# Windowed attention and an ELU feed-forward on one core: the last product's bank copied out by ScalarE, the other sums added from SBUF

## The chip, the cores and the metric

The kernel runs on one core of a Trainium2 chip. The metric is device time in microseconds of one launch. The engines are TensorE (PE, with its weight loads as PEld), VectorE (DVE), ScalarE (ACT), GpSimd (POOL) and SyncE (SP), which issues the DMAs. Each works through its own queue in order and waits on semaphores for the others.

## The reference

For 8 batches and 8 heads, 512 local and 32 global positions, head dimension 64. Global queries see all keys; local queries see the 32 global keys and local keys at most 32 positions away. The 4352 rows of 512 that come out go through two dense layers with an ELU between them.

```python
s_g = scale * q_g @ concat(k_g, k_l).T          # 32 rows per head
out_g = softmax(s_g) @ concat(v_g, v_l)
s_l = concat(scale * q_l @ k_g.T, where(abs(i - j) <= 32, scale * q_l @ k_l.T, -1e9))
out_l = softmax(s_l) @ concat(v_g, v_l)
x = concat(out_g, out_l)                        # to [4352, 512], rows by batch and position
h = x @ w_in                                    # w_in [512, 2048]
g = where(h > 0, h, exp(min(h, 0)) - 1)
out = g @ w_out                                 # w_out [2048, 512]
```

## The kernel before

The rows are worked in 17 blocks of 256 (16 of local rows and one that gathers all global rows). The dense products are done in fp16 parts: each operand is split into a high and a low half, and a product is three matmuls (high by high, high by low, low by high).

For a block, `ffn1` makes 256 columns of h at a time (eight steps `p`): 24 matmuls into a bank called `h`. ScalarE makes `g` (relu, then exp) and `hs` from it, VectorE joins them and forms sums and differences of quarters (`gs`), ScalarE rounds these to the high halves `gh`, and VectorE makes the low halves `gl`. Two steps later `ffn2` takes them to the second product. The first four blocks are done while the weights arrive, in groups of steps, with partial sums parked in DRAM (`od`). The other 13 use `ffn2_seven`: the second product as seven products of 128x128 by 128x256 quarters (Strassen's scheme with sums of quarters), kept over all eight steps in four PSUM banks that stay with it from the first such block on: two of the tiles named `acc`, one named `h`, one named `pa`. Bank `i` holds the products of `SEVEN[i]`, two in each of the first three and the last product alone in `acc[3]` (on rows of the profile: `pa<-cu,gh` and `pa<-cu,gl`). At the last step (`p == NP - 1`) ScalarE copies the first three banks to SBUF tiles `e` (named `tmp`), and functions `s0`, `s1`, `s2` put the four quarters of the output together on VectorE.

PSUM tiles come from three pools: `ps_h` (2 banks), `ps_o` (2) and `ps_a` (4, name `pa`). With `ffn2_seven`'s four taken, one bank is left of `ps_h` and three of `ps_a`; those three serve, in turn, the scores, their transposes, and the product with V.

Attention is a generator of slots that yields between its parts. For each slot `stage_s` (or `stage_ga` for the global rows) makes scores (`pa<-k,q`, `pa<-k,qg`), two slots later `stage_t` transposes the probabilities (`pa<-ident,p`) and VectorE or ScalarE copies them to `pt`, and three slots later `stage_v` multiplies by V (`pa<-pt,v`). For the global rows, `top` finds the maxima (`mg`), `ex` the exponentials `pg` with their sums, and `norm` divides (`sg`, then `pk` and `pg` on GpSimd). `split_x` rounds a finished block of attention output to `xh` and `xl` for ffn1; `scales` makes the factors `xs` of a job on GpSimd; `add_up` forms sums of quarters of w_out (`cu<-wouth,woutl` on GpSimd, then `tmp`).

What orders the work: a loop at the end draws from the attention generator and, by the table `PACE`, from the feed-forward generator, and calls `tick()` after each yield of the latter. `defer(n, fn)` puts `fn` n ticks later. Once the tables of group "f" are there (`pin[0]`), every engine keeps the order in which the program emits; before, a scheduler may reorder. A tick in the middle of the kernel is mostly six matmuls. Most instructions are recorded under line 63, the helper that emits them, so they are told apart by their tiles.

## Time and profile before

| | |
|---|---|
| median of 3 runs | 1060.09 us (1059.58 to 1062.56) |
| profiled execution | 1058.33 us, span 1056.5 us |
| mean granted TensorE clock | 0.975 |
| busy: PE / PEld / DVE / ACT / POOL | 92% / 73% / 75% / 63% / 26% |
| last block without attention beside it | from about 929 us on |
| last matmul, end of the span | about 1043.4 us, 1056.5 us |

A row of a timeline gives the start, the duration in us, engine, line, operation, output<-inputs with shapes and the number of merged instructions; in brackets, how long the engine stood idle before it and what let it go. A row of the waits gives the engine that waited, the one it waited for, the total in us, the number of times and the longest. A row of the groups gives busy time and the mean of one in ns, then idle time ahead. DMA rows are not needed here: the DMA engines' share is low after 400 us.

### The profile page before, as it was taken

Reading aid. Unit: us, or ns where it says so; the run is one execution under the profiler, and the core shown is the slowest. Engines: PE = TensorE matmul, PEld = TensorE weight load, DVE = VectorE, ACT = ScalarE, POOL = GpSimd, SP = SyncE. Lnnn points to the kernel's source line nnn. Section 1 sums busy time; section 2 is a strip of 40 time slices with the busy share of each in tenths; the row PEclk is TensorE's granted clock in tenths of the full one; section 3 lists DMA queues with packets and bytes.
Section 4 is the critical chain, followed back from the end, with each engine's and each line's share of the span. In section 5 each row is a group of like instructions: output and inputs, shape, how many; then the busy total and the mean of one; then the engine's idle time right before and its main releaser. Section 6 shows DMA issues by size and latency. Waiting matters only on the chain.

```text
span 1056.5 us, 21611 instructions
## 1 busy us (share of the span) xinstructions
PE 973.8 (92%) x8128; PEld 776.0 (73%) x8128; DVE 793.2 (75%) x2217; ACT 664.5 (63%) x1535; POOL 271.6 (26%) x458
## 2 busy tenths in 40 slices
PE   6898879887999999989999998999999998999994
PEld 4576546665676688877887787878888887888883
DVE  5789899986886877767776777686886877666663
ACT  4779767764655666555665666566746665656563
POOL 3446484164434321101111121021211221100000
PEclk8899989999999999999999999999999999999998
DMA  7536665430321122002210123012210000000000
GB/s 265 178 109 232 228 218 192 157 116 34 112 65 47 40 76 101 26 11 96 76 46 16 41 76 101 21 35 78 76 41 21 31 21 31 1 21 21 1 21 21
DMA packets 39169, 81.96 MB, mean 78 GB/s; under 512 B 3864, under 2 KB 5912, under 8 KB 39064
## 3 DMA queue, kind: packets, MB, share of 16 engines
q1 hardware_dynamic: 39064, 80.58, 22.7%
q8 instruction: 64, 1.05, 0.4%
q14 instruction: 41, 0.34, 0.1%
HBM read 65.36 MB, written 15.20 MB: 76 GB/s over the span
## 4 chain that ended last, share of the span: by engine, by line
PE 60%; DVE 21%; ACT 11%; issue 3%; POOL 3%; DMA 1%; DVEq 0%; POOLq 0%; ACTq 0%
PE h L63 27%; PE pa L63 20%; PE acc L63 12%; DVE o L63 4%; ACT gh L63 3%; DVE cu L63 3%; DVE gl L63 3%; ACT g L63 2%; DVE g L63 2%; DVE p L63 2%; DVE gs L63 1%; ACT p L63 1%; POOL cu L63 1%; ACT xh L63 1%; DVE woutl L63 1%
## 5 line engine op out<-in xcount | busy, mean ns | idle before, releaser
L63 PE MATMUL h<-xh,winh 128*128 128x256 f16 x992 | 273.6, 276 | 5.8 <-ACT xh L63 5.8
L63 PE MATMUL h<-xl,winh 128*128 128x256 f16 x992 | 273.3, 276 | 0.1
L63 PE MATMUL h<-xh,winl 128*128 128x256 f16 x992 | 273.2, 275 | 0.0
L63 POOL TENSOR_SCALAR p<-p,sm 128x224 f32<-128x224 f32 x256 | 139.7, 563 | 466.8 <-DVE sm L63 273.2
L63 PEld LDWEIGHTS <-winh 128*128 128x128 f16 x2176 | 213.3, 99 | 44.9 <-issue 14.2
L63 PEld LDWEIGHTS <-gh 128*128 128x128 f16 x1712 | 166.7, 99 | 68.6 <-issue 29.0
L63 ACT ACTIVATE g<-h,xs 128x512 f32<-128x512 f32 x124 | 85.0, 686 | 178.2 <-PE h L63 178.0
L63 DVE SCALAR_TENSOR_TENSOR gl<-g,xs,gh 128x256 f16<-128x256 f32 (+1 forms) x136 | 81.5, 599 | 96.8 <-ACT gh L63 96.1
L63 ACT ACTIVATE p<-p,m 128x224 f32<-128x224 f32 x256 | 120.7, 478 | 16.1 <-DVE m L63 15.7
L63 PEld LDWEIGHTS <-winl 128*128 128x128 f16 x1088 | 107.5, 99 | 13.8 <-issue 0.4
L63 PE MATMUL acc<-wouth,gh 128*128 128x256 f16 (+1 forms) x336 | 109.1, 325 | 7.9 <-DVE o L63 6.5
L63 PEld LDWEIGHTS <-gl 128*128 128x128 f16 x856 | 83.9, 98 | 34.7 <-DVE gl L63 6.9
L63 PE MATMUL acc<-wouth,gl 128*128 128x256 f16 (+1 forms) x336 | 106.3, 316 | 2.6 <-DVE gl L63 2.5
L63 PE MATMUL acc<-woutl,gh 128*128 128x256 f16 (+1 forms) x336 | 106.2, 316 | 0.0
L63 DVE TENSOR_TENSOR gs<-g 128x256 f32<-128x256 f32 (+1 forms) x312 | 102.1, 382 | 3.6
L63 DVE SCALAR_TENSOR_TENSOR gl<-gs,xs,gh 128x640 f16<-128x640 f32 x104 | 92.8, 893 | 15.9 <-ACT gh L63 15.5
L63 DVE SCALAR_TENSOR_TENSOR g<-g,hs 128x512 f32<-128x512 f32 x136 | 97.7, 719 | 4.8 <-ACT g L63 4.8
L63 ACT ACTIVATE gh<-g,xs 128x256 f16<-128x256 f32 (+1 forms) x136 | 75.5, 555 | 33.3 <-DVE g L63 32.4
L63 PE MATMUL pa<-ident,p 128*128 128x128 f32 x512 | 79.6, 282 | 14.0 <-ACT pg L63 5.8
L63 ACT ACTIVATE gh<-gs,xs 128x640 f16<-128x640 f32 x104 | 85.6, 823 | 2.0 <-DVE gs L63 1.9
L63 ACT ACTIVATE g<-g 128x512 f32<-128x512 f32 x136 | 85.5, 629 | 0.0
L63 ACT ACTIVATE hs<-h,xs 128x512 f32<-128x512 f32 x124 | 84.4, 681 | 0.0
(169 smaller groups left out, 1812.5 us busy)
## 6 DMA issues: line engine op xcount, KB each, us to landing
v<-vT SPq DMA_DIRECT2D x64, 256.0 KB, 2.7
k<-kT SPq DMA_DIRECT2D x32, 448.0 KB, 3.6
out<-o SPq DMA_DIRECT2D x34, 256.0 KB, 2.2
q<-qT SPq DMA_DIRECT2D x32, 256.0 KB, 5.3
raw<-w_in SPq DMA_DIRECT2D x8, 1024.0 KB, 6.5
raw<-w_out SPq DMA_DIRECT2D x8, 1024.0 KB, 5.1
od<-o SPq DMA_DIRECT2D x24, 256.0 KB, 2.3
o<-od SPq DMA_DIRECT2D x24, 256.0 KB, 3.2
```

The source lines that it names most:

```text
L63: ins = getattr(self.engine, name)(*args, **kwargs)
```

## The change

At the last step ScalarE also copies the bank of the last product, scaled, into two quarters of the output tiles (`c11` and `c22`) as soon as its matmuls are issued. VectorE forms the remaining sums in the SBUF tiles `m4` and `m6` and adds these to `c11` and `c22`; before, it read the bank itself in the last two operations. The output tiles are taken at that earlier point. And for global rows `ex` and `norm` are deferred by 3 and 6 ticks rather than 4 and 7.

```diff
                 if p == NP - 1 and i < 3:
                     nc.scalar.activation(e[i].rearrange("p a b -> p (a b)"), acc[i], AF.Copy, scale=oc)
+                elif p == NP - 1:
+                    o = [ffn.tile([P, DM], F32, name="o", bufs=3) for _ in range(2)]
+                    c11, c12, c21, c22 = (o[t][:, c:c + 256] for t in range(2) for c in (0, 256))
+                    for c in (c11, c22):
+                        nc.scalar.activation(c, acc[3][:, 0:256], AF.Copy, scale=oc)
                 yield
             if p == NP - 1:
-                o = [ffn.tile([P, DM], F32, name="o", bufs=3) for _ in range(2)]
                 (m6, m3), (m7, m4), (m2, m5) = ((x[:, 0, :], x[:, 1, :]) for x in e)
-                c11, c12, c21, c22 = (o[t][:, c:c + 256] for t in range(2) for c in (0, 256))
 
                 def s0():
+                    nc.vector.tensor_add(c21, m2, m4)
                     nc.vector.tensor_sub(c12, m5, m3)
-                    nc.vector.tensor_sub(c11, m4, m7)
-                    nc.vector.tensor_sub(c11, c11, m5)
+                    nc.vector.tensor_sub(m4, m4, m7)
 
                 def s1():
-                    nc.vector.tensor_sub(c22, m6, m3)
-                    nc.vector.tensor_sub(c22, c22, m2)
-                    nc.vector.tensor_add(c21, m2, m4)
+                    nc.vector.tensor_sub(m4, m4, m5)
+                    nc.vector.tensor_sub(m6, m6, m3)
+                    nc.vector.tensor_sub(m6, m6, m2)
 
                 def s2():
-                    for t, c in enumerate((c11, c22)):
-                        nc.vector.scalar_tensor_tensor(out=c, in0=acc[3][:, 0:256], scalar=oc, in1=c,
-                                                       op0=ALU.mult, op1=ALU.add)
+                    for t, (c, m) in enumerate(((c11, m4), (c22, m6))):
+                        nc.vector.tensor_add(c, c, m)
                         nc.sync.dma_start(out_rows(blk, t), o[t])
...
             if pin[0]:
-                for i, fn in ((1, top), (4, ex), (7, norm)):
+                for i, fn in ((1, top), (3, ex), (6, norm)):
                     defer(i, fn)
```

TensorE's order is the same in both. VectorE at the end of the first seven-product block (near 410 us; `tmp` are the copied banks, `o` the output tiles, `pt` the transposed probabilities, `mg` the maxima of global rows):

```order
 L63 TENSOR_TENSOR o<-tmp 128x256 x2
-L63 TENSOR_TENSOR o<-o,tmp 128x256
-L63 TENSOR_TENSOR o<-tmp 128x256
-L63 TENSOR_TENSOR o<-o,tmp 128x256
-L63 TENSOR_TENSOR o<-tmp 128x256
-L63 COPY pt<-pa 128x4x128
-L63 SCALAR_TENSOR_TENSOR o<-pa,xs,o 128x256 x2
+L63 TENSOR_TENSOR tmp<-tmp 128x256 x4
+L63 COPY pt<-pa 128x4x128
+L63 TENSOR_TENSOR o<-o,tmp 128x256 x2
 L63 TENSOR_REDUCE mg<-pa 128x1 x2
```

The eight operations stay eight and keep their places, ahead of and behind the copy to `pt`; the last two no longer name the bank `pa`. On ScalarE the two copies `o<-pa` stand behind `tmp<-h`, at most a few exponentials `p` or copies `pt` and `xr` later. ScalarE's order near 452 us, before and then after:

```order
L63 ACTIVATE gh<-g,xs 128x256
L63 ACTIVATE gh<-gs,xs 128x640
L63 ACTIVATE xh<-xr,xm 128x1024
L63 ACTIVATE pg,sg<-pa,mg 128x272 x2
L63 COPY pt<-pa 128x4x32
```

```order
L63 ACTIVATE gh<-g,xs 128x256
L63 ACTIVATE gh<-gs,xs 128x640
L63 ACTIVATE pg,sg<-pa,mg 128x272 x2
L63 ACTIVATE xh<-xr,xm 128x1024
L63 COPY pt<-pa 128x4x32
```

`pg` and `xh` change places here and near 572 us; at the other six global rows' places after 405 us they keep theirs. GpSimd's order near 330 us (`xs` are the scales of the first seven-product job, `cu` sums of w_out's quarters):

```order
 L63 MEMSET pt 96x4x32
-L63 TENSOR_SCALAR xs<-isc,xm 128x8 x2
-L63 TENSOR_SCALAR xs<-t_f,xm 128x8
-L63 TENSOR_SCALAR xs<-wm_f,xm 128x1
-L63 TENSOR_SCALAR pk<-pg,sg 128x32
-L63 TENSOR_SCALAR pg<-pg,sg 128x4x128
+L63 TENSOR_SCALAR pk<-pg,sg 128x32
+L63 TENSOR_SCALAR pg<-pg,sg 128x4x128
+L63 TENSOR_SCALAR xs<-isc,xm 128x8 x2
+L63 TENSOR_SCALAR xs<-t_f,xm 128x8
+L63 TENSOR_SCALAR xs<-wm_f,xm 128x1
 L63 TENSOR_TENSOR cu<-wouth,woutl 128x1024 x2
```

The scales move behind `pk` and `pg`. Near 300 us one `cu` moves behind `pk` and `pg` in the same way.

## The prediction

> **What bounds the kernel now.** I read the page's busy time first, then the list of who waited for whom (TensorE's part), then the timeline of each engine around every place where TensorE stood still after 405 us.

> ```profile
> PE 973.8 (92%) x8128; PEld 776.0 (73%) x8128; DVE 793.2 (75%) x2217; ACT 664.5 (63%) x1535; POOL 271.6 (26%) x458
> PE pa L63 <- DVE o L63: 13.5, 10, 3.0
> ```

> TensorE is the bound. Its longest wait in total is the one that the change aims at: ten times, 13.5 us together, the first matmul into bank `acc[3]` (tile `pa`) of a new block stood until VectorE had done the last two operations on `o`, which read that bank. In the stage without attention three of these waits follow one another:

> ```profile
> 929.19 0.38 PE L63 MATMUL pa<-cu,gh 128*128 128x256 f16 x2 [1.19 <-DVE o L63]
> ...
> 970.32 0.38 PE L63 MATMUL pa<-cu,gh 128*128 128x256 f16 x2 [1.35 <-DVE o L63]
> ...
> 1011.45 0.38 PE L63 MATMUL pa<-cu,gh 128*128 128x256 f16 x2 [1.35 <-DVE o L63]
> 965.74 0.70 ACT L63 ACTIVATE tmp<-h,xs 128x512 f32<-128x512 f32 x1
> ```

> **Term 1, the boundaries without attention: -3.9 us.** ScalarE finished `tmp<-h` of the boundary at 970 at 965.74 + 0.70 = 966.44, and in the new order the two copies of bank 3 come next on it. Nothing shows these copies; the nearest rows are a copy of the same size out of PSUM and, as an upper end, the 128x512 one above (0.70 each):

> ```profile
> L63 ACT COPY xr<-pa 128x256 f32<-128x256 f32 x54 | 20.4, 378 | 17.0 <-PE pa L63 17.0
> L63 DVE TENSOR_TENSOR o<-o,tmp x26: 424/425/569, 411.2 to 1045.4; 128x256 f32<-128x256 f32 x26
> L63 DVE SCALAR_TENSOR_TENSOR o<-pa,xs,o x26: 453/472/479, 413.4 to 1046.5; 128x256 f32<-128x256 f32 x26
> ```

> I take 0.38 each, since size and source are the same, so 0.75 for both (at most 1.4). The bank is then free at about 967.2 to 967.8. TensorE comes to it at 970.32 - 1.35 = 968.97 without the wait, so nothing of the wait is left: 1.19 + 1.35 + 1.35 = 3.9 us. ScalarE's own 0.75 us per block lies in time in which it is ahead of TensorE here. VectorE runs eight operations as before; the two that read PSUM (0.472) become adds from SBUF (0.425), about 0.1 us less per block, at most 0.15 each more where an add runs as the slowest one above (0.569).

> **Term 2, the boundaries with attention: -4.5 us of 9.6.** 13.5 - 3.9 = 9.6 us of the waits lie there, in seven places. After `acc[3]` TensorE comes to the product with V (`pa<-pt,v`), at once or after half of an ffn1. That product needs the second `pt` copy of VectorE: it reads it, and its output takes the bank that the copy empties. VectorE issues this copy next to the same `o` operations. So TensorE is let go by `o` only to meet `pt`. Pairs of copy and product, boundary by boundary, VectorE's and then TensorE's timeline:

> ```profile
> 475.91 0.68 DVE L63 COPY pt<-pa 128x512 f32<-128x512 f32 x1
> ...
> 533.46 0.67 DVE L63 COPY pt<-pa 128x512 f32<-128x512 f32 x1
> ...
> 594.80 0.67 DVE L63 COPY pt<-pa 128x512 f32<-128x512 f32 x1
> ...
> 653.20 0.68 DVE L63 COPY pt<-pa 128x512 f32<-128x512 f32 x1
> ...
> 711.27 0.68 DVE L63 COPY pt<-pa 128x512 f32<-128x512 f32 x1
> ...
> 768.15 0.66 DVE L63 COPY pt<-pa 128x512 f32<-128x512 f32 x1
> ...
> 881.16 0.66 DVE L63 COPY pt<-pa 128x512 f32<-128x512 f32 x1
> ```

> ```profile
> 477.84 1.21 PE L63 MATMUL pa<-pt,v 128*64 128x160 f32 x16
> ...
> 534.19 1.21 PE L63 MATMUL pa<-pt,v 128*64 128x160 f32 x16
> ...
> 595.52 1.21 PE L63 MATMUL pa<-pt,v 128*64 128x160 f32 x16
> ...
> 654.41 1.21 PE L63 MATMUL pa<-pt,v 128*64 128x160 f32 x16
> ...
> 712.48 1.21 PE L63 MATMUL pa<-pt,v 128*64 128x160 f32 x16
> ...
> 769.72 1.21 PE L63 MATMUL pa<-pt,v 128*64 128x160 f32 x16
> ...
> 881.01 0.38 PE L63 MATMUL pa<-cu,gh 128*128 128x256 f16 x2 [3.04 <-DVE o L63]
> ...
> 882.74 1.21 PE L63 MATMUL pa<-pt,v 128*64 128x160 f32 x16
> ```

> At 534.19 and 595.52 the product already starts 0.06 and 0.05 us after the copy's end (534.13, 595.47): there the gain is only what VectorE is sooner, 0.15 each. Elsewhere the gain is the product's start less the copy's end and 0.06: 477.84 - 476.65 = 1.2; 654.41 - 653.94 = 0.5; 712.48 - 712.01 = 0.5; 769.72 - 768.87 = 0.85; 882.74 - 881.88 = 0.85. With 0.1 us less on VectorE at the last four, 1.2 + 0.15 + 0.15 + 0.6 + 0.55 + 0.95 + 0.9 = 4.5 us. At 881 the wait of 3.04 us thus turns into one of some 2.1 us on `pt`. The ends: 0, where the next thing on VectorE binds as well, and 9.6. ScalarE's 0.75 us is covered here too: it makes `g`, `hs`, `gh` later by that much, and their readers (`gl` on VectorE, and TensorE when it reuses the only free `h` bank) come later than that, with the least to spare at 881, where `hs` would end about when TensorE wants the bank; there TensorE is to wait for `pt` anyway. The output DMAs on SP stand behind the same last operations as before.

> **Term 3, the softmax of the global rows one tick sooner: -4.7 us.** ScalarE's order changes at two of the eight places after 405 us: `xh` now comes behind the two `pg` activations (at 452 and 572).

> ```profile
> 446.84 0.77 DVE L63 TENSOR_REDUCE mg<-pa 128x1 f32<-128x272 f32 x2
> 451.17 1.15 ACT L63 ACTIVATE xh<-xr,xm 128x1024 f16<-128x1024 f32 x1 [1.59 <-DVE xm L63]
> 452.22 0.47 ACT L63 ACTIVATE pg<-pa,mg 128x272 f32<-128x272 f32 x1
> 452.93 0.82 PE L63 MATMUL pa<-ident,p 128*128 128x128 f32 x4 [2.34 <-ACT pg L63]
> ...
> 572.57 0.99 PE L63 MATMUL pa<-ident,p 128*128 128x128 f32 x4 [2.35 <-ACT pg L63]
> ```

> The maxima (`mg`) were long there; ScalarE stood 1.59 us for `xm` with `pg` queued behind. In the new order `pg` runs in that idle time, from about 449.6, and frees TensorE's bank by 450.3, before TensorE wants it (452.93 - 2.34 = 450.59). `xh` still starts when `xm` is there, with room for the two `pg` ahead of it. So both waits go: 2.34 + 2.35 = 4.7 us, unless VectorE's next `pt` copy, which is not sooner, holds TensorE in turn (then down to 0):

> ```profile
> 455.60 0.67 DVE L63 COPY pt<-pa 128x512 f32<-128x512 f32 x1
> ```

> ```profile
> 459.52 1.03 PE L63 MATMUL pa<-k,q 64*128 64x224 f32 x8
> ```

> It ends at 456.27; the scores that need its bank come at 459.52 - 2.34 = 457.18 or later, 0.9 us behind it, so I keep the whole.

> **Term 4, GpSimd's queue: +1.0 us.** The same edit puts `pk` and `pg` on GpSimd ahead of the first seven-product job's scales (`xs`).

> ```profile
> 329.82 1.33 POOL L63 TENSOR_SCALAR xs<-isc,xm 128x8 f32<-128x8 f32 x2
> ...
> 331.36 0.26 POOL L63 TENSOR_SCALAR xs<-wm_f,xm 128x1 f32<-128x1 f32 x1
> 338.43 0.29 POOL L63 TENSOR_SCALAR pk<-pg,sg 128x32 f32<-128x32 f32 x1 [6.81 <-DVE sg L63]
> ...
> 341.94 0.69 DVE L63 TENSOR_TENSOR tmp<-cu 128x512 f32<-128x512 f32 x1 [2.68 <-POOL cu L63]
> ```

> The scales ran in GpSimd's idle time; now they wait behind `pk` for `sg`, and `cu`, for which VectorE already stood 2.68 us, comes behind them. They took 331.62 - 329.82 = 1.8 us, the last of the four 0.26: 1.0 to 1.8 for four. VectorE, which has hardly a gap for some 15 us from there, then holds TensorE through `pt`. I take 1.0 (0 to 2.7, a repeat of VectorE's wait). At the other place where GpSimd's order changes (`cu` behind `pk`, `pg` near 300 us) TensorE shows no wait, so I put nothing. The tail, after the last matmul, gains 0.1.

> **Sum:** -3.9 - 4.5 - 4.7 + 1.0 - 0.1 = -12.2 us. The profiled execution took 1058.33 us (span 1056.5) and would take 1046.1. It is 1.8 us under the median of the runs, 1060.09; against that I forecast 1047.9 us.

> [...] GpSimd's `p` scalings run beside these VectorE operations at several boundaries:

> ```profile
> L63 POOL TENSOR_SCALAR p<-p,sm 128x224 f32<-128x224 f32 x256 | 139.7, 563 | 466.8 <-DVE sm L63 273.2
> ```

> The dependent adds from SBUF quoted above, some of them beside such scalings, took 0.569 at the worst and 0.425 in the median. [...]

> **The rivals.**
> 1. *All of the waits go*: VectorE also gets to `pt` sooner, or the product was not bound by it. Then -13.5 - 4.7 + 1.0 - 0.1 = -17.3, 1042.8 us. For it: the group row. Against: the two starts 0.05 us behind the copy.
> 2. *The waits in the attention stages only change their name*: `pt` and other VectorE work hold TensorE there for as long, and what is won at 452 and 572 is given back to `pt`. Only the stage without attention gains: -3.9 - 0.1 + 1.0 = -3.0, 1057.1 us. For it: VectorE is busy without a gap around each boundary. Against: it has gaps later in every block.
> [...]

> **Chances.** The forecast 0.58; rival 1 0.12; rival 2 0.15; rival 3 0.10, of which 0.04 for the part that makes it slower; 0.05 for none of these. What this kernel's measurement can tell from no change is about 0.3%, 3.2 us, so rival 2 lies at its edge. Faster 0.83, same 0.11, slower 0.06. The range goes from rival 1 to beyond rival 3 with one scaling and near rival 2: 1042.5 to 1055.5 us.

> **What would show it.** Right: no wait of `pa` for `o` on TensorE; one for `pt` that grows from little to some 4 us, the largest at the boundary near 870; the three late blocks 39.8 us apart instead of 41.1; no wait of TensorE for `pg` near 450 and 560. Wrong: adds of `o` over 0.6 us (rival 3), TensorE waiting for `hs` or `gl` after a boundary (ScalarE's 0.75 us not covered), or a wait of over 2 us near 340 (term 4 too small).

## The result and the profile after

| | before | changed |
|---|---|---|
| median of four runs each, us | 1060.62 (1059.58 to 1062.56) | 1046.75 (1044.79 to 1048.67) |
| ratio of times, 95% interval | | 0.9867 (0.9843 to 0.9891) |
| profiled execution, us | 1058.33 | 1044.79 |
| its span, us | 1056.5 | 1043.0 |

The forecast was 1047.9 us, 12.2 us less than before; the profiled execution became 13.5 us shorter. From the page of the changed kernel, the busy time, and from the list of waits TensorE's rows (us in total, times, the longest):

```profile
PE 970.9 (93%) x8128; PEld 774.2 (74%) x8128; DVE 790.9 (76%) x2217; ACT 673.9 (65%) x1561; POOL 273.4 (26%) x458
PE pa L63 <- DVE pt L63: 9.0, 13, 1.4
PE pa L63 <- ACT pg L63: 1.1, 1, 1.1
```

The row "pa <- DVE o" (13.5 us, ten times) no longer exists. ScalarE has 26 instructions and 9.4 us more, the copies of the bank. Two rows that the prediction did not show stood in the kernel before as follows:

```profile
PE pa L63 <- DVE pt L63: 2.0, 3, 1.4
PE pa L63 <- ACT pg L63: 5.8, 3, 2.4
```

So 13.5 us of waits for `o` and 4.7 for `pg` went, and 7.0 us of waits for `pt` came; 5.35 of these stand at the product with V behind the boundaries, where the prediction expected some 4. TensorE's timeline shows some of the new waits at that product, and, last, the uses of the bank in the stage without attention, which have no wait in brackets any more and are 39.62 us apart (41.13 before):

```profile
343.48 0.77 PE L63 MATMUL pa<-pt,v 128*64 128x160 f32 x8 [0.57 <-DVE pt L63]
...
475.55 1.21 PE L63 MATMUL pa<-pt,v 128*64 128x160 f32 x16 [1.35 <-DVE pt L63]
...
872.64 0.71 PE L63 MATMUL pa<-pt,v 128*64 128x160 f32 x8 [0.59 <-DVE pt L63]
...
874.17 0.71 PE L63 MATMUL pa<-pt,v 128*64 128x160 f32 x8 [0.82 <-DVE pt L63]
...
958.40 0.38 PE L63 MATMUL pa<-cu,gh 128*128 128x256 f16 x2
...
998.02 0.38 PE L63 MATMUL pa<-cu,gh 128*128 128x256 f16 x2
```

**Where the time went, piece by piece.** TensorE runs the same 8128 matmuls in the same order in both kernels, so the n-th of one can be set against the n-th of the other. The change of the difference of their starts over a stretch is what the stretch gained or lost. In us, by stretches of the kernel before; the last two rows are the first two experiments below:

| against before | 0-300 | 300-400 | 400-500 | 500-600 | 600-700 | 700-800 | 800-900 | 900-end |
|---|---|---|---|---|---|---|---|---|
| changed kernel | -0.5 | +2.33 | -4.13 | -3.18 | -0.59 | -1.54 | -1.46 | -4.36 |
| bank copy only | -3.0 | +1.59 | -0.92 | -0.32 | -0.57 | -1.53 | -1.45 | -4.35 |
| ticks only | +0.4 | +2.32 | -1.62 | -2.86 | +0.01 | +0.02 | +1.61 | +0.02 |

The first column is what executions differ by anyway: two kernels below that are the same up to 405 us differ by up to 2.6 us there. Behind 300 us stretches that run the same work agree to 0.02 us, so that one profiled execution resolves tenths of a microsecond there, with one exception: up to 405 us the kernel with the bank copy only is the kernel before, and yet it lost 1.59 us between 300 and 400 us. It has a window at half the TensorE clock there (near 360 us) that the kernel before has not; such windows come up again below, and a single execution can have one more or one less of them. The changed kernel gained 12.9 us behind 300 us: +2.33 (term 4), -6.05 (term 3: -3.19 around 452 and -2.86 around 572, and the ticks alone show the same two), -4.85 (term 2, what is left of 400 to 900; the bank copy alone shows 4.8) and -4.36 (term 1).

### The profile page after: what moved, and what is told of

Same layout as the page of the kernel before. It is cut to its first block, busy times and chain, and to the rows that moved or that the text cites. A ratio compares the mean times of both kernels' runs of the same rounds, so it can differ in the third digit from the quotient of the medians.

```text
span 1043.0 us, 21668 instructions
## 1 busy us (share of the span) xinstructions
PE 970.9 (93%) x8128; PEld 774.2 (74%) x8128; DVE 790.9 (76%) x2217; ACT 673.9 (65%) x1561; POOL 273.4 (26%) x458
## 4 chain that ended last, share of the span: by engine, by line
PE 60%; DVE 22%; ACT 11%; issue 3%; POOL 3%; DMA 1%; SPq 0%; DVEq 0%; POOLq 0%; ACTq 0%
PE h L63 27%; PE pa L63 21%; PE acc L63 13%; DVE cu L63 3%; DVE gl L63 3%; ACT gh L63 3%; DVE g L63 2%; ACT g L63 2%; DVE tmp L63 2%; DVE p L63 2%; ACT p L63 1%; DVE gs L63 1%; DVE o L63 1%; POOL cu L63 1%; DVE xl L63 1%
## 5 line engine op out<-in xcount | busy, mean ns | idle before, releaser
L63 PE MATMUL h<-xh,winh 128*128 128x256 f16 x992 | 271.6, 274 | 5.8 <-ACT xh L63 5.8
L63 PE MATMUL h<-xl,winh 128*128 128x256 f16 x992 | 271.3, 274 | 0.1
L63 PE MATMUL h<-xh,winl 128*128 128x256 f16 x992 | 271.3, 273 | 0.0
L63 POOL TENSOR_SCALAR p<-p,sm 128x224 f32<-128x224 f32 x256 | 142.7, 577 | 456.0 <-DVE sm L63 257.5
L63 PEld LDWEIGHTS <-winh 128*128 128x128 f16 x2176 | 211.8, 99 | 43.8 <-issue 14.4
L63 PEld LDWEIGHTS <-gh 128*128 128x128 f16 x1712 | 166.9, 99 | 54.5 <-issue 13.7
L63 ACT ACTIVATE g<-h,xs 128x512 f32<-128x512 f32 x124 | 85.1, 687 | 168.0 <-PE h L63 164.9
L63 DVE SCALAR_TENSOR_TENSOR gl<-g,xs,gh 128x256 f16<-128x256 f32 (+1 forms) x136 | 82.3, 605 | 88.9 <-ACT gh L63 88.2
L63 ACT ACTIVATE p<-p,m 128x224 f32<-128x224 f32 x256 | 120.7, 478 | 15.7 <-DVE m L63 15.3
L63 PE MATMUL acc<-wouth,gh 128*128 128x256 f16 (+1 forms) x336 | 109.1, 325 | 8.7 <-DVE o L63 6.6
L63 PEld LDWEIGHTS <-winl 128*128 128x128 f16 x1088 | 106.8, 98 | 13.1 <-issue 0.4
L63 PEld LDWEIGHTS <-gl 128*128 128x128 f16 x856 | 84.1, 98 | 35.2 <-DVE gl L63 7.4
L63 PE MATMUL acc<-wouth,gl 128*128 128x256 f16 (+1 forms) x336 | 106.3, 316 | 3.1 <-DVE gl L63 3.0
L63 PE MATMUL acc<-woutl,gh 128*128 128x256 f16 (+1 forms) x336 | 106.2, 316 | 0.0
L63 DVE TENSOR_TENSOR gs<-g 128x256 f32<-128x256 f32 (+1 forms) x312 | 102.1, 381 | 3.6
L63 DVE SCALAR_TENSOR_TENSOR gl<-gs,xs,gh 128x640 f16<-128x640 f32 x104 | 92.6, 890 | 15.5 <-ACT gh L63 15.1
L63 DVE SCALAR_TENSOR_TENSOR g<-g,hs 128x512 f32<-128x512 f32 x136 | 96.0, 706 | 4.6 <-ACT g L63 4.6
L63 ACT ACTIVATE gh<-g,xs 128x256 f16<-128x256 f32 (+1 forms) x136 | 75.9, 558 | 31.6 <-DVE g L63 30.8
L63 ACT ACTIVATE gh<-gs,xs 128x640 f16<-128x640 f32 x104 | 86.0, 827 | 2.5 <-DVE gs L63 2.4
L63 PE MATMUL pa<-ident,p 128*128 128x128 f32 x512 | 79.4, 280 | 8.5 <-POOL p L63 3.4
L63 ACT ACTIVATE g<-g 128x512 f32<-128x512 f32 x136 | 85.9, 631 | 0.0
L63 ACT ACTIVATE hs<-h,xs 128x512 f32<-128x512 f32 x124 | 84.7, 683 | 0.0
```

The source lines that it names most:

```text
L63: ins = getattr(self.engine, name)(*args, **kwargs)
```

## The experiments

**1. The bank copy alone.** The changed kernel with the ticks of before:

```
-                for i, fn in ((1, top), (3, ex), (6, norm)):
+                for i, fn in ((1, top), (4, ex), (7, norm)):
```

> Only the bank copy, its sums and adds; the exponentials of the global rows and their normalisation stay at ticks 4 and 7. Theory (the parts add, each as the two traces show it): the three late boundaries give 1.3 + 1.5 + 1.5 = 4.3 us, the seven in attention 4.3 us net, the tail 0.1: 8.7 us under the kernel before, about 1051.9 us. The waits of TensorE for `pg` near 452 and 572 us stay at 2.3 us each, and so do the two spells at half clock right behind them. Rival (the two parts need each other: with the exponentials behind `xh` the second copy on ACT delays them further): the pg waits grow by up to 0.9 us at each boundary and the gain shrinks to 5 us or less, about 1055.5 us.

Measured: 1049.83 us (1047.63 to 1051.7), ratio 0.9904 (0.9888 to 0.992) against 1059.73 us for the kernel before on this chip. The list of waits and TensorE's timeline at the place near 452:

```profile
PE pa L63 <- ACT pg L63: 5.8, 3, 2.3
```

```profile
451.49 0.85 PE L63 MATMUL pa<-ident,p 128*128 128x128 f32 x4 [2.34 <-ACT pg L63]
```

The waits for `pg` are as long as before, and the half-clock windows behind them are there (451.8 and 571.2 us). The late blocks gave 4.35 us and 400 to 900 us gave 4.8, against 4.3 expected of each. The theory holds; the rival falls. The 1.59 us between 300 and 400 us are not the copies' doing, as said above.

**2. The ticks alone.** The kernel before, with `(3, ex), (6, norm)`; the bank is read as before.

> Only the ticks: exponentials of the global rows at tick 3 and their normalisation at tick 6, the bank read as before. Theory: the two waits for `pg` near 452 and 572 us go, and with each the half-clock window behind it, in all 6.5 us; GpSimd's queue near 340 us costs 2.1 us back, part of it a new half-clock window near 364 us: 4.4 us under the kernel before, about 1056.2 us. Rival (the half-clock windows come and go by chance and do not belong to the wait): only the waits go, 4.7 us less 1 us, and the two half-clock windows are seen again near 453 and 573 us: 3.7 us or less, 1056.9 us.

Measured: 1058.67 us (1054.12 to 1060.41, 12 runs), ratio 0.9986 (0.9974 to 0.9998): nearly nothing. Both expectations missed the time. The waits for `pg` and the half-clock windows at 453 and 573 us are gone, as the theory said, and the cost near 340 is the same +2.32. But two waits that the kernel has always had are now followed by half-clock windows, which they were not before. Here is the one near 477 us, in windows of 3.41 us by the clock record's own borders (time, length, busy time and instructions of PE, PEld, DVE, ACT, POOL, then the granted clock). First the kernel before, then the ticks alone, and last TensorE's timeline of the ticks alone:

```profile
473.70:477.11 3.41, 1.52 (x12) 1.07 (x11) 3.34 (x9) 1.13 (x3) 2.82 (x4) 1.00 0.00 0
477.11:480.53 3.42, 3.10 (x34) 2.55 (x34) 3.38 (x13) 1.68 (x8) 0.00 (x0) 1.00 0.55 195
```

```profile
473.86:477.27 3.41, 1.21 (x10) 0.72 (x8) 3.38 (x10) 0.47 (x1) 2.29 (x4) 1.00 0.00 0
477.27:480.69 3.42, 3.42 (x24) 2.56 (x23) 3.35 (x12) 2.14 (x8) 0.00 (x0) 0.50 0.52 164
```

```profile
476.93 0.38 PE L63 MATMUL pa<-cu,gh 128*128 128x256 f16 x2 [2.20 <-DVE o L63]
```

The wait for `o` is the same (2.20 us here, 2.21 before). Before, a border cut it, and the window held 3.41 - 1.52 = 1.89 us of idle time; here it lies inside one window, 2.20 us, and the next window ran at a clock of 0.50. At 881 us the wait of 3.04 us does the same (1.92 us of it in one window before, 2.62 now). The table shows the price: 400 to 500 us gives 1.6 instead of 3.2, and 800 to 900 loses 1.61. With the 2.32 us near 340 they eat what the ticks gained. One of the 12 executions took 1054.12 us at a mean granted clock of 0.978, against 0.971 in the profiled one, so not every execution has as many half-clock windows. In the changed kernel these two waits do not exist. So the two parts of the change do need each other, though in another way than I had thought of: the ticks are worth 0.5 us alone and 5.4 us on top of the bank copy (both in the traces behind 300 us; 3.8 us if the bank copy's trace had not had its own window near 360 us).

**3. The normalisation back at tick 7**, the exponentials left at tick 3.

```
-                for i, fn in ((1, top), (3, ex), (6, norm)):
+                for i, fn in ((1, top), (3, ex), (7, norm)):
```

> The changed kernel with the normalisation back at tick 7 and the exponentials left at tick 3, so that GpSimd scales `xs` ahead of `pk` and `pg` again in front of the first job of seven products. Theory (the term of GpSimd's queue cost 2.1 us there): the wait of ACT for `xs` near 339 us falls from 3.0 us to under 1 us, the half-clock window near 364 us goes, the waits for `pg` at 452 and 572 us stay away since ACT's order decides them: 2 us under the changed kernel, about 1044.7 us. Rival (the tick of the normalisation is what brought `pg` in time): 2.4 to 3.2 us come back at each of 452 and 572 us, and the kernel is 2 to 4 us over the changed one, 1049 us or more.

Measured: 1042.55 us (1042.05 to 1045.52), ratio 0.9842 (0.9824 to 0.986); against the changed kernel's trace -2.33 us between 300 and 400 us and 0.00 to the end. ScalarE's row in the changed kernel and in this one:

```profile
339.33 0.69 ACT L63 ACTIVATE g<-h,xs 128x512 f32<-128x512 f32 x1 [3.01 <-POOL xs L63]
```

```profile
336.94 0.69 ACT L63 ACTIVATE g<-h,xs 128x512 f32<-128x512 f32 x1 [1.02 <-PE h L63]
```

The wait for `xs` and TensorE's 0.57 us for `pt` at 343 are gone, and with them the half-clock window at 364. The wait for `gl` in front of that window is the same length in both kernels:

```profile
362.17 0.28 PE L63 MATMUL acc<-wouth,gl 128*128 128x256 f16 x1 [2.03 <-DVE gl L63]
```

```profile
361.07 0.28 PE L63 MATMUL acc<-wouth,gl 128*128 128x256 f16 x1 [2.01 <-DVE gl L63]
```

What differs is where it falls: one window holds 2.07 us of idle time in the changed kernel and 1.36 here. It does not look like chance: with the exponentials early, the four traces with GpSimd's new order (the changed kernel, 2, 4 and 6) hold 2.07 to 2.10 us there and all have the window, the five with the old order (3, 5, 7, 8 and 9) hold 1.30 to 1.46 and none has it. But it is not the kernel alone that decides: with both ticks as before, the kernel before has none there (1.20 us), and the bank copy alone, the same program up to there, has one (2.16 us idle in the window, its +1.59 in the table). The waits for `pg` stay away: ScalarE's order decides them.

**4. The sums later.** The changed kernel, with the three groups of sums nine ticks further back:

```
-                    defer(1 + i, fn)
+                    defer(10 + i, fn)
```

> The changed kernel with the three groups of sums put off by nine ticks more, behind the `pt` copies and `gl` on VectorE. Theory (what is late after the change is `pt`, behind the sums of VectorE: 5.35 us of waits of V at the seven boundaries in attention): most of these waits go, 3 to 5 us under the changed kernel, about 1043 us. Rival (`pt` is late because of the softmax chain itself, or the sums now stand in front of something as urgent, `gl` or the next `o`): 0 to 1 us, or slower by up to 2 us through waits for `gl` or `o` that are not there now.

Measured: 1040.77 us (1038.99 to 1042.57), ratio 0.9819 (0.9801 to 0.9837); against the changed kernel's trace -6.25 us behind 300 us, all of it between 400 and 900. VectorE's timeline at the first boundary, in the changed kernel and in this one, and this one's row in the list of waits:

```profile
472.11 0.18 DVE L63 RECIPROCAL sm<-sm 128x4 f32<-128x4 f32 x1
472.20 0.74 DVE L63 TENSOR_TENSOR o<-tmp 128x256 f32<-128x256 f32 x2
472.86 2.03 DVE L63 TENSOR_TENSOR tmp<-tmp 128x256 f32<-128x256 f32 x4
474.82 0.68 DVE L63 COPY pt<-pa 128x512 f32<-128x512 f32 x1
```

```profile
473.62 0.18 DVE L63 RECIPROCAL sm<-sm 128x4 f32<-128x4 f32 x1
473.71 0.66 DVE L63 COPY pt<-pa 128x512 f32<-128x512 f32 x1
```

```profile
PE pa L63 <- DVE pt L63: 3.6, 6, 1.4
```

The copy that TensorE waits for came 2.71 us behind the reciprocal because six sums, which nobody was waiting for, stood between. Put off, they cost nothing: the waits for `pt` fall from 9.0 to 3.6 us, none of them is at V behind a boundary, and no wait for `gl` or `o` takes their place. The gain is above the 3 to 5 us expected.

**5. Both together** (experiments 3 and 4).

> The sums put off and the normalisation back at tick 7, both in the changed kernel. Theory (two separate places: V behind `pt` at the seven boundaries, ACT behind `xs` near 339 us): the two gains add, 2.6 us (with no half-clock window near 364 us) under the kernel with the late sums alone: about 1038.5 us, and no half-clock window between 270 us and the end. Rival (with the sums behind `gl` the normalisation at tick 7 finds VectorE busy and `pg` comes late): no better than the late sums alone, 1040.8 us or more.

Measured: 1036.77 us (1036.01 to 1038.97), ratio 0.9797 (0.9783 to 0.9811) against 1058.26 us on this chip; -8.55 us against the changed kernel's trace behind 300 us (-2.32 and -6.23). The clock record shows no half-clock window between 268 and 1025 us. The gains add, and this is the fastest version that was run.

**6. The copies made twice.** The changed kernel:

```
-                    for c in (c11, c22):
+                    for c in (c11, c22, c11, c22):
```

> The changed kernel with both copies of the bank made twice, two more ACT instructions of 0.36 us pitch at each of 13 ends, which also hold the bank 0.7 us longer. Theory (the copies lie beside TensorE's work; between the second copy's end and the next use of the bank near 919 us there are 1.8 us): within 1 us of the changed kernel, and the late blocks stay 39.6 us apart. Rival (ACT's chain behind the copies, `g`, `hs`, `gh`, or the exponentials in attention, comes last): each of the ten binding ends pays up to 0.7 us, 4 to 7 us in all, the late blocks 40.3 us apart.

Measured: 1047.26 us (1046.68 to 1048.26), ratio 0.9894 (0.988 to 0.9907), an interval that overlaps the changed kernel's. The traces are sharper: behind 300 us TensorE's matmuls differ by 0.01 us from the changed kernel's, in sum and in each stretch. Near 870 TensorE first waits 0.6 us for `hs`, and then as much less for `pt`. ScalarE's copies are covered at all 13 ends, and made twice they still cost nothing; near 870 that is so only because `pt` comes later still.

**7. VectorE reads the bank first**, on top of experiment 5; no copies on ScalarE.

```
-                    for c in (c11, c22):
-                        nc.scalar.activation(c, acc[3][:, 0:256], AF.Copy, scale=oc)
+                    for c, m in ((c11, e[1][:, 1, :]), (c22, e[0][:, 0, :])):
+                        nc.vector.scalar_tensor_tensor(out=c, in0=acc[3][:, 0:256], scalar=oc, in1=m,
+                                                       op0=ALU.mult, op1=ALU.add)
```

> On top of the late sums with tick 7: no ACT copies; VectorE reads the bank at once instead, adding M4 and M6 as it does (c11 = bank + M4, c22 = bank + M6), and the other sums are taken from the output tile later. Theory (what counts is that the bank is read first, by whichever engine): within 1.5 us of the kernel with both, about 1038 us; ACT has 0.85 us less at each end. Rival (VectorE's two reads of some 0.55 us stand ahead of `g`, `gs` and `gl`, or behind other work of VectorE, so that the bank is let go later): 0.5 to 1 us at each of ten ends, 1043 to 1048 us.

Measured: 1038.34 us (1037.55 to 1039.06), ratio 0.9807 (0.9794 to 0.982). Against experiment 5's trace it is +1.33 us behind 300 us, at one place: the scores at 585 us, which wait for VectorE's `sm`, behind the two reads.

```profile
585.06 0.99 PE L63 MATMUL pa<-k,q 64*128 64x224 f32 x6 [1.58 <-DVE sm L63]
```

So what counts is that the bank is read first, and hardly which engine does it; ScalarE, with more room, is the slightly better one.

**8 and 9. Waits made on purpose.** On top of experiment 5, each pair of copies is repeated so that ScalarE holds the bank longer, by another amount at each of the 13 ends; `n` counts the ends.

```
-                    for c in (c11, c22):
+                    n = state["n7"] = state.get("n7", -1) + 1
+                    for c in (c11, c22) * (1 + (2, 3, 4, 5)[n % 4]):
```

> A kernel made to wait: late sums with tick 7, and the pair of bank copies repeated 2, 3, 4, 5, 2, 3, ... times more at the 13 ends, so that ACT holds the bank 1.4 to 3.6 us longer and TensorE idles for graded times there (time 1045 to 1065 us; only the trace counts). Theory (the clock is set by fixed windows of 3.41 us; one in which TensorE idles for about 2.0 us or more is followed by one at half clock): each wait of over 2.0 us inside one window is followed by a half-clock window that costs up to 1.7 us, and a wait of the same length that is cut by a window's border is not. Rival 1 (only a window that is idle from end to end counts): no half-clock window behind any wait under 3.4 us. Rival 2 (no tie to waits): half-clock windows stand where TensorE did not wait, as often as behind waits. [...]

Measured: 1050.49 us (one run). The waits came out shorter than meant, 1.9 us at most for `o` and no window after 265 us with over 1.55 us of idle time; no half-clock window appeared. That agrees with the theory and with rival 1, and tells nothing apart, so the series was made longer, with (5, 6, 7, 8, 9)[n % 5]:

> The same made longer: the pair of copies repeated 5, 6, 7, 8, 9, 5, ... times more at the 13 ends, so that the bank is let go 3.6 to 6.5 us later and TensorE waits for `o` for 1.5 to over 4 us (time 1060 to 1095 us; only the trace counts). By the windows counted in the runs so far the next window ran at half clock whenever TensorE was idle for 2.07 us or more of one (nine windows after 265 us), and never when it was idle for 1.92 us or less. Theory (that share decides, wherever in the window the idle time lies): every window after 265 us with over 2.1 us of idle time is followed by a half-clock one, none with under 1.9 us is, and waits of the same length fall on either side by where the border cuts them. Rival (only a window that is idle from end to end): half-clock windows only behind waits that hold a whole window, over 3.4 us, at most a few here.

Measured: 1092.47 us (one run). Four windows, each with the one behind it:

```profile
657.43:660.84 3.41, 0.74 (x6) 0.51 (x6) 0.00 (x0) 3.41 (x10) 0.00 (x0) 1.00 0.03 11
660.84:664.26 3.42, 3.42 (x24) 2.36 (x22) 2.48 (x7) 1.39 (x4) 0.00 (x0) 0.50 0.00 0
...
995.34:998.75 3.41, 1.52 (x14) 1.13 (x12) 0.00 (x0) 3.41 (x10) 0.00 (x0) 1.00 0.00 0
998.75:1002.17 3.42, 3.36 (x31) 2.77 (x30) 1.85 (x3) 3.01 (x6) 0.00 (x0) 1.00 0.00 0
```

```profile
473.11:476.52 3.41, 1.54 (x19) 1.16 (x18) 0.29 (x3) 3.41 (x9) 0.23 (x1) 1.00 0.00 0
476.52:479.94 3.42, 3.42 (x19) 2.43 (x18) 2.65 (x5) 3.30 (x12) 0.00 (x0) 0.50 0.26 81
...
950.97:954.38 3.41, 0.00 (x0) 0.00 (x0) 0.00 (x0) 3.41 (x11) 0.00 (x0) 1.00 0.00 0
954.38:957.80 3.42, 2.77 (x14) 1.98 (x14) 0.49 (x2) 3.38 (x7) 0.00 (x0) 0.50 0.02 5
```

All six windows at full clock with 2.14 to 3.41 us of idle time (2.28 at 592.57, 2.67 at 657.43 and 3.41 at 950.97 among them) were followed by one at half clock, and only the one at 950.97 is idle from end to end: the rival falls. The border is not sharp: 1.87 us (473.11) was enough, against what I expected, and 1.89 us (995.34) was not.

## Why the prediction held, and where its steps failed

**Term 1 (boundaries without attention): -4.36 us, forecast -3.9.** Mechanism and place as forecast. The three waits gave 1.35, 1.51 and 1.51 us, 0.16 more each than their rows (1.19, 1.35, 1.35). The reason is how a wait is counted:

```profile
968.70 0.27 PE L63 MATMUL h<-wouth,gl 128*128 128x256 f16 x1
970.32 0.38 PE L63 MATMUL pa<-cu,gh 128*128 128x256 f16 x2 [1.35 <-DVE o L63]
```

```profile
958.29 0.27 PE L63 MATMUL h<-wouth,gl 128*128 128x256 f16 x1
958.40 0.38 PE L63 MATMUL pa<-cu,gh 128*128 128x256 f16 x2
```

The wait is counted from the modelled end of the matmul ahead, 968.70 + 0.27. Without it the next one starts 0.11 us after that matmul's start, as the changed kernel's second pair shows: 1.62 - 0.11 = 1.51. A matmul's printed length is not its pitch, the time from one start to the next.

**Term 2 (boundaries with attention): -4.85 us, forecast -4.5.** The reading that TensorE is let go by `o` only to meet `pt` was right: of 9.6 us of waits for `o` about half was gained. This is shown, not only argued, by experiment 4, which took the cause of the new waits away and gained another 6.25 us. The shares were less exact than the sum: 0.94 us at 477 instead of 1.2, and 1.47 at 881 instead of 0.9; the other five came within 0.03. At 477 VectorE's six sums ahead of `pt` had become slower. They took 2.35 us from their first start to the copy's before (473.56, below, to 475.91) and 2.62 in the changed kernel (472.20 to 474.82), which is the 0.26 us that are missing:

```profile
473.56 0.74 DVE L63 TENSOR_TENSOR o<-tmp 128x256 f32<-128x256 f32 x2
```

Rival 1 (all of the waits go) needed the sums out of `pt`'s way, which this change did not do; in experiment 4 the seven places gave 11.1 us together, which is all of their waits when each is counted as in term 1.

**Term 3 (softmax of the global rows): -6.05 us, forecast -4.7.** Both waits went, as said, and gave 2.5 us each. Two sizes failed. The window behind each wait had run at half clock, which the prediction did not look for. In the kernel before and in the changed one:

```profile
453.22:456.64 3.42, 3.42 (x19) 2.48 (x17) 2.95 (x9) 0.32 (x3) 0.79 (x2) 0.50 0.00 0
```

```profile
453.00:456.40 3.40, 3.40 (x33) 3.10 (x32) 2.18 (x3) 2.93 (x6) 0.00 (x0) 1.00 0.00 0
```

At half clock 19 matmul instructions fit, at full clock 33; that was 1.7 us at each place. And "I keep the whole" was wrong. TensorE comes to the scores 4.2 us sooner, not 2.34, and so ahead of the `pt` copy, which is not sooner. VectorE's and then TensorE's timeline in the changed kernel:

```profile
457.44 1.27 DVE L63 COPY pt<-pa 128x512 f32<-128x512 f32 x2
```

```profile
458.17 1.02 PE L63 MATMUL pa<-k,q 64*128 64x224 f32 x6 [0.37 <-DVE pt L63]
```

The waits for `pt` are 0.37 us here and 0.71 near 573 by their rows, and by the starts 1.00 and 1.35 us were given back.

**Term 4 (GpSimd's queue): +2.3 us, forecast +1.0.** What the term named, V's wait for `pt`, cost 0.7 us; VectorE's wait for `cu` grew by only 0.3 us, to 2.98. The rest, 1.6 us, is the half-clock window at 364, which this small delay triggered by moving a wait of 2.0 us against the border (experiment 3: 2.07 us of idle time in one window with the delay, 1.36 without).

**ScalarE's copies** took 0.49 us each and 0.85 a pair, not 0.38 and 0.75: the COPY row of the same size was not the right one for an ACTIVATE with a scale. It changed nothing (experiment 6).

**Slow adds (rival 3)** came in a small form: none took over 0.6 us, the sign that was set for them. The copies and the final adds in the changed kernel (min/median/max in ns):

```profile
L63 ACT ACTIVATE o<-pa,xs x26: 454/493/510, 412.1 to 1030.6; 128x256 f32<-128x256 f32 x26
L63 DVE TENSOR_TENSOR o<-o,tmp x26: 395/416/584, 415.5 to 1033.0; 128x256 f32<-128x256 f32 x26
```

The slowest add lost 0.17 us against the median; eight of the 26 ran beside a scaling, and six of these lost nothing. So no add lost the length of a whole scaling, and the row with 0.569 was a fair guide to the size. Some sums do lose time beside a scaling, though. Ten of VectorE's sums and adds in the changed kernel end 0.27 us behind the end of the scaling that ran when they started, and the scalings beside the sums and adds take 0.61 to 0.87 us, against mostly 0.45 elsewhere. In experiment 5 a pair of adds met the longer scaling `pg` and took 1.22 us, 0.48 more than a pair without a scaling. Here GpSimd's row in experiment 5, VectorE's pair of adds beside it, and a pair without a scaling in the changed kernel:

```profile
419.29 0.69 POOL L63 TENSOR_SCALAR pg<-pg,sg 128x512 f32<-128x512 f32 x1
419.36 1.22 DVE L63 TENSOR_TENSOR o<-o,tmp 128x256 f32<-128x256 f32 x2
...
475.42 0.74 DVE L63 TENSOR_TENSOR o<-o,tmp 128x256 f32<-128x256 f32 x2
```

The sums ahead of `pt` meet scalings as well: at 477 the third and the fourth of the six took 0.59 and 0.56 us, against 0.47 and 0.41 for the third and the fourth before, and there the 0.26 us were lost.

The sum came out close partly by luck: the errors of terms 3 (-1.35 us) and 4 (+1.33) have opposite signs.

## What to carry to other kernels

When a wait is removed, ask what stands next on the releasing engine's queue: work that nobody needs yet (here six sums) ahead of work that is needed at once (`pt`) keeps half of the wait alive under another name, and putting it off may be worth more than the change itself. Price a wait of TensorE from the start of the matmul ahead plus its pitch (0.11 us here), and look at the granted clock in the window behind it: here a wait of 2.20 us (477, experiment 2) and one of 3.04 us (881) each cost 1.6 us more by the half-clock window behind them. Do not add up parts of a change that were timed apart when such windows can move from one wait to another.

## What the runs showed of the hardware

The clock was the surprise. In the eleven traces together, after 265 us and as long as TensorE had work left, each of 17 full-clock windows of 3.41 us in which TensorE was idle for 2.07 us or more was followed by a window at a clock of 0.50; with 1.92 us or less the next stayed at 1.00, but for the one of 1.87 us. The 17 are two in the kernel before, one in the changed kernel, three each in experiments 1 and 2, one each in 4 and 6, and six in 9. Such a half-clock window cost 1.6 to 1.7 us where TensorE had work for all of it. In the traces of the two kernels, from their start on, a half-clock window with 0.74 us of idle time or more was itself followed by another, seven times of seven before the last matmul (0.97 us at 262.07 in the kernel before, 1.29 us at 261.42 in the changed one); behind those with 0.28 us or less, and behind the one at 954.38 in experiment 9 with 0.64 us, the clock was full again.

The place of a wait against these borders is regular behind 300 us, although the starts of the executions are not. Taking off what each trace is late at 300 us (the first column of the table above), the clock record's border near 262 us lies between 261.8 and 262.1 us in ten of the eleven traces. In the bank copy alone the borders lie about 1.7 us off that, and this is the trace with a half-clock window near 360 us that the kernel before has not. It stays open why the place is the same in ten and not in that one; it was not tried.
